# First loads of an adaLN block issued by SyncE and ScalarE in turn, and ScalarE's function table loaded behind its issues

## The chip, the cores and the metric

One core of a Trainium2 chip runs the kernel: TensorE (PE), VectorE (DVE), ScalarE (ACT), GpSimd (POOL) and SyncE (SP), which here only issues DMAs. The metric is the device time of one execution in microseconds (us), lower is better. It was 543.92 us as the median of three runs (543.61 to 544.06).

## What is computed

One transformer block whose layer norms are modulated by a condition c. The sizes are S = 2048 tokens, D = 512, 32 heads of 16, F = 1376; everything is f32. Cut to what matters:

```python
mod = (silu(c) @ w_mod).reshape(1, 6, 1, 512)
sa, ca, ga, sb, cb, gb = mod's six rows
h = layernorm(x) * (1 + ca) + sa
q, k, v = split(h @ wqkv)                 # 32 heads of 16
phi = lambda t: where(t > 0, t + 1, exp(t)) + 1e-6
kv, z = einsum("sd,se->de", phi(k), v), phi(k).sum(tokens)      # per head
x = x + ga * ((phi(q) @ kv / (phi(q) . z + 1e-6)) @ wo)
h = layernorm(x) * (1 + cb) + sb
x = x + gb * (((h @ w_gate) * (h @ w_up)) @ w_down)
```

The change touches only how the first inputs come in: x, c, and the columns of w_mod for ca and sa.

## The kernel before

The program is written in a fixed order (a manual schedule): each engine runs its instructions in the order in which the code emits them, and waits at an instruction until its operands are there. The tokens are cut into four chunks (NCH) of four tiles (NJ) of 128 tokens, the 512 features into four blocks (KD) of 128. f32 operands of the large products are split into a high and a low part (`split`, L195, the high part by ScalarE at L196, the low part by VectorE at L197), and each product is three matmuls.

**Loads (L111 to L135).** `load` takes a tile and issues one DMA of 256 KB from SyncE's queue. All loads of the first stage are emitted one after the other: four x tiles of chunk 0 (in what follows x0 to x3), c (`ct`, 2 KB), four row groups of w_mod for ca (`raw_ca`), four for sa (`raw_sa`), then the K columns of wqkv (`raw_k`), x of chunk 1, the Q and V columns, and x of chunks 2 and 3.

**The opening (L432 to L505).** TensorE starts with 24 dummy matmuls (`keep_on(24)`, L146, whose operand VectorE makes at L140 and L141), and more of them stand between the first transposes. Meanwhile

- VectorE takes the statistics of the four x tiles as they land (L244, L245); GpSimd makes rstd (L265), VectorE nmr (L269);
- ScalarE normalises a tile (`xhat`, L274) as soon as nmr is there. Between its first and second tile stands exp(-c) (`silu_exp`, L153), from which VectorE makes sc = silu(c) (L156 to L158);
- VectorE and ScalarE sum the rows of w_mod with the weights sc: acc_ca with L164 and three L166, acc_sa with ScalarE's L446, two L166, and the last row group by TensorE itself (L468);
- TensorE transposes the normalised tiles (L302), then turns acc_ca and acc_sa into columns by a product with ones (L459 for ca; L468 and L469 for sa). VectorE takes the columns out (L176, L492), makes the first modulated block (L494), and the first projection starts (K, L489, then L482 to L484).

From there the K projection, the key-value sums, Q, the attention output and the feed-forward part follow.

**ScalarE's function table.** The load of the table (ACT_TABLE_LOAD) is placed by the compiler ahead of the first ACTIVATE on ScalarE's queue, which before is that of the first `xhat`, L274.

Of the kernel before, what the change touches and what calls it, by code (L numbers as in the profile page):

```python
# [8 lines left out]
F32 = mybir.dt.float32  # L9
F32R = mybir.dt.float32r  # L10
AF = mybir.ActivationFunctionType
# [3 lines left out]
P = 128  # L15
# [9 lines left out]
def tile_adaln_block(  # L25
# [12 lines left out]
    nc = tc.nc  # L38
    ctx.enter_context(tc.manual_schedule())
    _, S, D = x.shape  # L40
    F = w_gate.shape[1]
    KD = D // P
    NJ = 4
# [9 lines left out]
    xv = x[0].rearrange("(c p j) d -> c j p d", p=P, j=NJ)  # L53
# [5 lines left out]
    wm_v = w_mod.rearrange("(p k) n -> p k n", k=KD)  # L59

    pool = lambda name, bufs, **kw: ctx.enter_context(tc.tile_pool(name=name, bufs=bufs, **kw))
    consts = pool("consts", 1)
# [14 lines left out]
    def B(tag, shape=(P, D), dt=F32):  # L77

        return T(tiles, tag, shape, dt)
# [28 lines left out]
    nc.gpsimd.memset(half, -0.5)  # L108


    def load(src, tag):  # L111
        raw = B(tag, (P, *src.shape[1:]))[:src.shape[0]]
        nc.sync.dma_start(raw, src)
        return raw

    def load_x(ch):
        return [load(xv[ch, j], "x") for j in range(NJ)]

    def load_mod(v):
        return [load(wm_v[:, k, v * D:(v + 1) * D], "raw") for k in range(KD)]  # L120

    def load_qkv(n):
        return [load(wqkv_v[k, :, n * D:(n + 1) * D], "raw") for k in range(KD)]

    xts = [load_x(0)]
    ct = consts.tile([P, KD], F32, name="ct")
    nc.sync.dma_start(ct, c[0].rearrange("(p k) -> p k", k=KD))
    raw_ca = load_mod(1)
    raw_sa = load_mod(0)
    raw_k = load_qkv(1)  # L130
    xts.append(load_x(1))
    raw_q = load_qkv(0)
    raw_v = load_qkv(2)
    xts.append(load_x(2))
    xts.append(load_x(3))  # L135

# [407 lines left out]
    def mod_load(*vs):  # L544
        raw_m.update({v: load_mod(v) for v in vs})
# [25 lines left out]
    for i in range(NT):  # L571
        ch, j = divmod(i, NJ)
# [1244 lines left out]
```

## Time and profile before

| what | before |
|---|---|
| median of three runs | 543.92 us |
| the profiled execution, its own time | 543.86 us |
| its span, first to last instruction | 542.2 us |
| instructions | 8140 |
| granted TensorE clock, mean | 1.0 |
| bytes by DMA, mean rate | 109.21 MB, 201 GB/s |

The profile is of one execution. Busy times are sums over an engine's instructions; a view by stages cuts the span at given times; the view of waits says for how long an engine stood still ahead of an instruction and what ended that; the timeline gives for each instruction, or for a run of the same ones, the start, the time from the first start to the last end, the engine, the line and the tiles. For a DMA the last number of its row is the time from its issue to its landing. A row "PEld" is a weight load on TensorE, which may run beside the matmul ahead of it. Times are counted from the start of the span.

### The profile page before, as it was taken

To read this page: it belongs to the slowest core of one execution; us is meant where nothing else is said; L and a number is where in the kernel's file an instruction comes from. 1 tells how busy PE (TensorE), PEld (TensorE's weight loads), DVE (VectorE), ACT (ScalarE), POOL (GpSimd) and SP (SyncE) were. 2 spreads that over 40 slices of the span, in tenths; PEclk is the share of its full clock that TensorE was granted. 3 is DMA by queue.
4 is the path that set the end of the run, shared out by engine and by line. 5 is a ranking of instruction groups with operands and counts; after the bars stand their busy time and mean duration, and the time that the engine had idled before them with its cause. 6 is when DMAs were issued, how large, how long until landed. Compare 5 with 4: busy or idle time off the path is not lost. (4 is left out here: it accounts for less than half of the span.)

```text
span 542.2 us, 8140 instructions
## 1 busy us (share of the span) xinstructions
PE 535.5 (99%) x2617; PEld 448.3 (83%) x2617; DVE 407.4 (75%) x688; ACT 295.9 (55%) x557; POOL 160.7 (30%) x169
## 2 busy tenths in 40 slices
PE   8999999999999999999999999999999999999997
PEld 7888787888888878878888888887788888899996
DVE  7897779999989888779765677997745554666762
ACT  3696777648587765577674545444524234353320
POOL 2001010010021220085796566749622313210000
PEclk9999999999999999999999999999999999999999
DMA  8902427220165165947879496893189999689122
GB/s 280 383 35 98 136 93 218 89 68 2 44 195 196 37 213 154 294 142 237 285 215 314 186 318 207 254 371 95 43 299 375 380 382 325 224 296 365 52 79 78
DMA packets 86395, 109.21 MB, mean 201 GB/s; under 512 B 10896, under 2 KB 41616, under 8 KB 86352
## 3 DMA queue, kind: packets, MB, share of 16 engines
q1 hardware_dynamic: 86352, 108.70, 59.8%
q8 instruction: 20, 0.33, 0.2%
q14 instruction: 23, 0.19, 0.1%
HBM read 65.93 MB, written 42.73 MB: 200 GB/s over the span
## 5 line engine op out<-in xcount | busy, mean ns | idle before, releaser
L1156 PE MATMUL bank<-h,w 128*128 128x512 f32 (+1 forms) x630 | 145.7, 390 | 0.4 <-DVE u L1218 0.3
L1156 PEld LDWEIGHTS bank<-h,w 128*128 128x128 f32 (+1 forms) x630 | 116.9, 186 | 27.1 <-DVE u L1218 0.7
L1161 ACT ACTIVATE bank<-bank 128x512 f32<-128x512 f32 (+1 forms) x30 | 17.5, 583 | 73.8 <-PE bank L1156 73.6
L197 DVE TENSOR_TENSOR kl<-u,kh 128x512 fp32r<-128x512 f32 (+1 forms) x43 | 30.6, 743 | 27.8 <-ACT kh L196 23.7
L265 POOL TENSOR_TENSOR rstd<-ve,half 128x2 f32<-128x2 f32 (+3 forms) x13 | 11.8, 910 | 109.0 <-DVE ve L264 45.0
L211 PE MATMUL bank<-w,h 128*128 128x512 f32 x104 | 40.9, 393 | 0.1
L209 PE MATMUL bank<-w,h 128*128 128x512 f32 x104 | 40.9, 393 | 0.0
L210 PE MATMUL bank<-w,h 128*128 128x512 f32 x104 | 40.6, 390 | 0.0
L1156 PE MATMUL acc<-h,w 128*128 128x512 f32 x168 | 38.7, 389 | 0.0
L197 POOL TENSOR_TENSOR w<-raw,w 128x512 fp32r<-128x512 f32 (+1 forms) x15 | 21.6, 1446 | 53.4 <-ACT w L196 47.7
L873 PE MATMUL acc<-w,xh 128*128 128x512 f32 x120 | 37.1, 390 | 0.0
L1156 PEld LDWEIGHTS acc<-h,w 128*128 128x128 f32 x168 | 31.5, 188 | 6.5
L1118 POOL TENSOR_TENSOR w<-raw,w 128x256 fp32r<-128x256 f32 (+3 forms) x22 | 24.8, 1127 | 38.3 <-ACT w L1111 34.1
L943 DVE TENSOR_TENSOR x<-acc,x 128x512 f32<-128x512 f32 x40 | 26.1, 685 | 9.9 <-PE acc L1241 8.2
L1436 PE MATMUL acc<-w,kh 128*128 128x256 f32 (+1 forms) x176 | 31.9, 284 | 0.1
L1118 POOL TENSOR_TENSOR w<-t,w 128x512 fp32r<-128x512 f32 (+1 forms) x22 | 29.9, 1357 | 0.0
L196 ACT ACTIVATE kh<-u 128x512 fp32r<-128x512 f32 (+1 forms) x43 | 24.6, 622 | 8.3 <-DVE u L1413 8.3
L1436 PEld LDWEIGHTS acc<-w,kh 128*128 128x128 f32 (+1 forms) x176 | 27.5, 192 | 0.4 <-ACT kh L196 0.3
L873 PEld LDWEIGHTS acc<-w,xh 128*128 128x128 f32 x120 | 22.5, 188 | 4.6
L416 PE MATMUL acc<-kh,xh 128*128 128x512 f32 x64 | 25.3, 395 | 0.0
L1436 PE MATMUL acc<-w,kl 128*128 128x256 f32 x88 | 25.0, 284 | 0.2 <-DVE kl L197 0.2
L1436 PE MATMUL bank<-w,kh 128*128 128x256 f32 (+1 forms) x136 | 24.7, 284 | 0.5 <-DVE x L1485 0.5
(257 smaller groups left out, 1330.0 us busy)
## 6 DMA issues: line engine op xcount, KB each, us to landing
right<-w SPq DMA_DIRECT2D x56, 256.0 KB, 3.4
w<-right SPq DMA_DIRECT2D x56, 256.0 KB, 5.1
raw<-in_w_mod_dram SPq DMA_DIRECT2D x24, 256.0 KB, 3.7
raw<-in_B_w_down_dram SPq DMA_DIRECT2D x20, 256.0 KB, 4.4
down_t<-w SPq DMA_DIRECT2D x20, 256.0 KB, 5.1
w<-down_t SPq DMA_DIRECT2D x20, 256.0 KB, 4.2
x<-in_A_x_dram SPq DMA_DIRECT2D x16, 256.0 KB, 5.4
down_b<-w SPq DMA_DIRECT2D x15, 256.0 KB, 5.2
```

The costliest lines, as they stand in the source:

```text
L196: nc.scalar.activation(h, src, AF.Copy)
L197: (low or nc.vector).tensor_tensor(l, src, f32(h), op=ALU.subtract)
L209: nc.tensor.matmul(ps, ah, bh, start=i == 0, stop=False)
L210: nc.tensor.matmul(ps, ah, bl, start=False, stop=False)
L211: nc.tensor.matmul(ps, al, bh, start=False, stop=i == n - 1)
L416: nc.tensor.matmul(tacc[k], xh[:, a:b], kh, start=first, stop=False)
L873: nc.tensor.matmul(yps[i], x, y, start=False, stop=k == KD - 1 and x is al, skip_group_check=True)
L943: nc.vector.tensor_tensor(xt[:, a:b], dn[j][:, a:b], xt[:, a:b], op=ALU.add)
L1118: sub = lambda out, x, y: (on or nc.gpsimd).tensor_tensor(out, x, f32(y), op=ALU.subtract)
L1156: mm = lambda x, y, **kw: nc.tensor.matmul(ps, x[:, k], y, skip_group_check=True, **kw)
L1161: nc.scalar.activation(out, x, AF.Copy)
L1436: nc.tensor.matmul(ps, x[:, a:b], y, start=start, stop=False, skip_group_check=True)
```

## The change

`load` gets a parameter for the issuing engine, and `load_x` and `load_mod` one for a cycle of engines. For chunk 0 of x, for raw_ca and for raw_sa the tiles 0 and 2 are issued by SyncE and the tiles 1 and 3 by ScalarE; ct is issued by ScalarE. Behind these loads in the order of the program stands a new exp of a 128x1 tile on ScalarE, which is set to zero by VectorE ahead of L140. Later loads stay with SyncE.

```diff
-    def load(src, tag):
+    ONE, TWO = (nc.sync,), (nc.sync, nc.scalar)
+
+    def load(src, tag, by=nc.sync):
         raw = B(tag, (P, *src.shape[1:]))[:src.shape[0]]
-        nc.sync.dma_start(raw, src)
+        by.dma_start(raw, src)
         return raw
 
-    def load_x(ch):
-        return [load(xv[ch, j], "x") for j in range(NJ)]
+    def load_x(ch, by=ONE):
+        return [load(xv[ch, j], "x", by[j % len(by)]) for j in range(NJ)]
 
-    def load_mod(v):
-        return [load(wm_v[:, k, v * D:(v + 1) * D], "raw") for k in range(KD)]
+    def load_mod(v, by=ONE):
+        return [load(wm_v[:, k, v * D:(v + 1) * D], "raw", by[k % len(by)]) for k in range(KD)]
...
-    xts = [load_x(0)]
+    xts = [load_x(0, TWO)]
     ct = consts.tile([P, KD], F32, name="ct")
-    nc.sync.dma_start(ct, c[0].rearrange("(p k) -> p k", k=KD))
-    raw_ca = load_mod(1)
-    raw_sa = load_mod(0)
+    nc.scalar.dma_start(ct, c[0].rearrange("(p k) -> p k", k=KD))
+    raw_ca = load_mod(1, TWO)
+    raw_sa = load_mod(0, TWO)
+    early = consts.tile([P, 1], F32, name="early")
+    nc.vector.memset(early, 0.0)
+    nc.scalar.activation(early, early, AF.Exp)
     raw_k = load_qkv(1)
```

In the changed file the lines behind this place have numbers higher by 5 (L469 is L474 there).

How the instructions stand now is shown on three engines. In each row stand the line, the operation, the tile written and what is read (the numbers behind a name tell buffers apart), the shape, and the semaphores it waits for. DMAHW0 to DMAHW7 are eight semaphores which the loads take in turn, over both queues; a load that takes one again waits for the landing of the load that had it.

The start of SyncE's queue before: x_90 to x_96 are x0 to x3, raw_100 to raw_106 raw_ca, raw_108 to raw_114 raw_sa, raw_116 the first tile of raw_k.

```order
L113 DMA x_96<-in_A_x_dram 128x512
L127 DMA ct<-in_c_dram 128x4
L113 DMA raw_100<-in_w_mod_dram 128x512
L113 DMA raw_102<-in_w_mod_dram 128x512
L113 DMA raw_104<-in_w_mod_dram 128x512
L113 DMA raw_106<-in_w_mod_dram 128x512 [waits DMAHW0_49]
L113 DMA raw_108<-in_w_mod_dram 128x512 [waits DMAHW1_49]
L113 DMA raw_110<-in_w_mod_dram 128x512 [waits DMAHW2_49]
L113 DMA raw_112<-in_w_mod_dram 128x512 [waits DMAHW3_49]
L113 DMA raw_114<-in_w_mod_dram 128x512 [waits DMAHW4_49]
L113 DMA raw_116<-in_A_wqkv_dram 128x512 [waits DMAHW5_49]
```

DMAHW0 to DMAHW4 are those of x0, x1, x2, x3 and ct; the last tile of raw_sa (raw_114) waits for ct to land. The same stretch of SyncE's queue in the changed kernel (raw_119 is the first tile of raw_k there):

```order
L115 DMA x_90<-in_A_x_dram 128x512
L115 DMA x_94<-in_A_x_dram 128x512
L115 DMA raw_100<-in_w_mod_dram 128x512
L115 DMA raw_104<-in_w_mod_dram 128x512
L115 DMA raw_108<-in_w_mod_dram 128x512 [waits DMAHW1_49]
L115 DMA raw_112<-in_w_mod_dram 128x512 [waits DMAHW3_49]
L115 DMA raw_119<-in_A_wqkv_dram 128x512 [waits DMAHW5_49]
```

Seven loads have left SyncE's queue, and with them three of its waits. The start of ScalarE's queue before, with the first tile's xhat (n_216), exp (ce), the other tiles' xhat, and the first part of acc_sa (f_176):

```order
L274 ACT_TABLE_LOAD [waits DMAHW0_49]
L274 ACTIVATE n_216<-x_90,nmr_208,rstd_207 128x512 [waits DVE_49]
L153 ACTIVATE ce<-ct 128x4 [waits DMAHW4_49]
L274 ACTIVATE n_219<-x_92,nmr_208,rstd_207 128x512 [waits DMAHW1_49]
L274 ACTIVATE n_231<-x_94,nmr_208,rstd_207 128x512 [waits DMAHW2_49,DVE_49]
L274 ACTIVATE n_233<-x_96,nmr_208,rstd_207 128x512 [waits DMAHW3_49]
L446 ACTIVATE f_176<-raw_108,sc 128x512 [waits DMAHW1_49]
```

And in the changed kernel:

```order
L115 DMA x_92<-in_A_x_dram 128x512
L115 DMA x_96<-in_A_x_dram 128x512
L129 DMA ct<-in_c_dram 128x4
L115 DMA raw_102<-in_w_mod_dram 128x512
L115 DMA raw_106<-in_w_mod_dram 128x512 [waits DMAHW0_49]
L115 DMA raw_110<-in_w_mod_dram 128x512 [waits DMAHW2_49]
L115 DMA raw_114<-in_w_mod_dram 128x512 [waits DMAHW4_49]
L134 ACT_TABLE_LOAD
L134 ACTIVATE early<-early 128x1 [waits DVE_49]
L279 ACTIVATE n_219<-x_90,nmr_211,rstd_210 128x512 [waits DVE_49]
L158 ACTIVATE ce<-ct 128x4 [waits DMAHW5_49]
```

Seven issues now stand ahead of the table load, the new exp, the first xhat and exp of c, three of them with a wait for a landing. Which landing, the readers of the tiles show: DMAHW0 is x0's and DMAHW2 x2's, as before, and ct now has DMAHW5. Who has DMAHW4 is seen on VectorE, where sc and the first step of acc_ca (f_178) are made, in the changed kernel:

```order
L161 TENSOR_SCALAR ce<-ce 128x4 [waits Activation_49]
L162 RECIPROCAL ce<-ce 128x4 [waits DVE_49]
L163 TENSOR_TENSOR sc<-ct,ce 128x4 [waits DMAHW5_49,DVE_49]
L169 TENSOR_SCALAR f_178<-raw_100,sc 128x512 [waits DMAHW4_49,DVE_49]
L274 SCALAR_TENSOR_TENSOR nmr_211<-mv_176,rstd_210 128x2 [waits Pool_49]
```

DMAHW4 belongs to raw_100, the first tile of raw_ca, so ScalarE's last issue (raw_114) waits for raw_100 to land, where SyncE's before waited for ct.

## The prediction

> **What bounds the kernel now.** I read the share of busy time first, then TensorE by stages, then who it waits for.
>
> ```profile
> PE 535.5 (99%) x2617; PEld 448.3 (83%) x2617; DVE 407.4 (75%) x688; ACT 295.9 (55%) x557; POOL 160.7 (30%) x169
> ...
> 2.00:10.30 8.30, 8.30 (x24) 1.00 0.91 294
> 10.30:15.80 5.50, 5.50 (x46) 1.00 1.06 397
> 15.80:19.00 3.20, 3.20 (x15) 1.00 1.05 377
> 19.00:530.00 511.00, 510.18 (x2471) 1.00 0.60 200
> 530.00:542.20 12.20, 8.34 (x68) 1.00 0.26 87
> ```
>
> In the stage rows the columns are the stage, its length, TensorE's busy time with its instructions, the granted clock, the DMA share and GB/s. From 2.0 us on TensorE is busy to within 0.8 us until 530; the tail (3.9 us) belongs to the last outputs, which the change does not touch. The waits by TensorE say what could still be won:
>
> ```profile
> PE acc L146 <- DVE w L141: 2.0, 1, 2.0
> PE bank L1436 <- DVE x L1485: 0.5, 1, 0.5
> PE bank L1156 <- DVE u L1218: 0.3, 1, 0.3
> PE acc L1436 <- DVE kl L197: 0.2, 1, 0.2
> PE bank L1156 <- DVE u L1184: 0.2, 1, 0.2
> ```
>
> None of these is a wait for a load. The first is the start, the others sum to 1.2 us (0.5 + 0.3 + 0.2 + 0.2) and lie far behind the change. So TensorE's own queue is the bound, and a faster start of the data alone cannot pull it forward. That queue in the first 16 us:
>
> ```profile
> 2.00 8.48 PE L146 MATMUL acc<-w 128*128 128x512 f32 x24 [2.00 <-DVE w L141]
> 10.32 1.03 PE L302 MATMUL bank<-ident,n 128*128 128x128 f32 x8
> ...
> 12.99 1.00 PE L459 MATMUL acc<-ones,f 128*128 128x64 f32 x8
> 13.80 0.48 PE L146 MATMUL acc<-w 128*128 128x512 f32 x1
> 14.12 0.33 PE L468 MATMUL acc<-sc,raw 128*128 128x64 f32 x2
> 14.28 0.39 PE L469 MATMUL acc<-ones,f 128*128 128x64 f32 x2
> ...
> 15.86 1.24 PE L489 MATMUL acc<-w,h 128*128 128x512 f32 x4
> ...
> L459 PEld LDWEIGHTS acc<-ones,f x8: 190/192/192, 12.9 to 13.7; 128*128 128x128 f32 x8
> ...
> L469 PEld LDWEIGHTS acc<-ones,f x8: 192/192/192, 14.2 to 15.7; 128*128 128x128 f32 x8
> ```
>
> The columns are start, time from the first start to the last end, engine and line. The 24 dummy matmuls (L146) fill TensorE until 10.3, whatever the loads do; then transposes, column sums and the first projection (L489) follow with no gap. What must be ready is made by ScalarE and VectorE:
>
> ```profile
> 4.39 1.28 ACT L274 ACT_TABLE_LOAD   x1 [4.39 <-DMA x<-in_A_x_dram]
> 7.34 0.81 ACT L274 ACTIVATE n<-x,nmr,rstd 128x512 f32<-128x512 f32 x1 [1.67 <-DVE nmr L269]
> 8.06 0.19 ACT L153 ACTIVATE ce<-ct 128x4 f32<-128x4 f32 x1
> 8.16 0.80 ACT L274 ACTIVATE n<-x,nmr,rstd 128x512 f32<-128x512 f32 x1
> 9.71 1.52 ACT L274 ACTIVATE n<-x,nmr,rstd 128x512 f32<-128x512 f32 x2 [0.75 <-DVE nmr L269]
> 11.33 0.72 ACT L446 ACTIVATE f<-raw,sc 128x512 f32<-128x512 f32 x1
> 14.04 0.63 ACT L196 ACTIVATE w<-raw 128x512 fp32r<-128x512 f32 x1 [1.99 <-DMA raw<-in_A_wqkv_dram]
> ...
> 8.35 0.16 DVE L156 TENSOR_SCALAR ce<-ce 128x4 f32<-128x4 f32 x1
> ...
> 9.61 4.01 DVE L166 SCALAR_TENSOR_TENSOR f<-raw,sc,f 128x512 f32<-128x512 f32 x5
> ```
>
> The chain to follow is ce (ScalarE, ends 8.25), silu on VectorE from 8.35, and the five L166, which end at 13.62 with acc_sa. L469's first weight load, the first to read acc_sa, starts at 14.2 (14.23, since its matmul starts at 14.28 and the one before at 14.12). A reader starts some 0.1 us behind its source here (ce ends 8.25, VectorE 8.35), so acc_sa has about **0.5 us of slack**. The table load ends at 5.67, and ScalarE then waits 1.67 us for nmr: the table costs nothing today.
>
> **The change, part by part.** The table load, moved ahead of data that was waited for anyway, can win nothing; that is its best case. The new memset (128x1) stands ahead of VectorE's L140; its like, a 16-element operation such as L156, takes 0.16 us, so the first dummy starts at most 0.16 us later, and and what that moves on TensorE is covered by the wait found below: nothing, and up to 0.16 us if that wait is not there.
>
> The step that matters is the seven issues that now stand on ScalarE's queue ahead of the table load, exp and xhat. The order shown with the change says what they wait for: eight DMA semaphores go round over the loads of both queues, so a load waits for the landing of the one that had its semaphore before. ScalarE's fifth issue waits for x0, the sixth for x2, and the seventh, the last tile of raw_sa, for **the first tile of raw_ca** (raw_100). The same rule can be seen at work in the trace, on SyncE:
>
> ```profile
> x<-in_A_x_dram SPq DMA_DIRECT2D x1, 256.0 KB, 3.5
> x<-in_A_x_dram SPq DMA_DIRECT2D x1, 256.0 KB, 4.1
> x<-in_A_x_dram SPq DMA_DIRECT2D x1, 256.0 KB, 5.1
> 3.13 0.43 SPq L113 DMA_DIRECT2D raw<-in_w_mod_dram  x1
> raw<-in_w_mod_dram SPq DMA_DIRECT2D x1, 256.0 KB, 4.9
> 5.81 0.33 SPq L113 DMA_DIRECT2D raw<-in_w_mod_dram  x1
> 7.32 0.80 SPq L113 DMA_DIRECT2D raw<-in_w_mod_dram  x2
> SPq L113 <- DMA x<-in_A_x_dram: 1.5, 2, 1.2
> ```
>
> The x rows are x0, x2 and x3, issued at 0.81, 1.72 and 2.18, with the time to landing last: they land at 4.3, 5.8 and 7.3. The 11th and 12th issue start at 5.81 and 7.32, right behind x2 and x3. Until now such waits stood on SyncE, which computes nothing. Now one stands ahead of everything that ScalarE does. raw_100, issued at 3.13, lands today at 3.13 + 4.9 = 8.0, later than ScalarE's first xhat begins (7.34).
>
> When will it land? It is now the third issue of SyncE's queue, where x2 stood (1.72). Early bound: with the shortest landing of any row, 3.5, it is there at 5.2. Late bound: the four x tiles still go ahead of it on the same DMA engines, and a w_mod tile of ScalarE's queue now goes beside it; a tile takes 0.65 us of the engines (256 KB at 397 GB/s), so 8.0 + 0.65 = 8.7. The landings are further apart (4.3, 5.8 and 7.3 for x0, x2 and x3) than the issues, so the transfer sets the pace, and what an earlier issue wins and the tile beside it costs I set against each other: **8.0**, as today.
>
> (The Trainium skill, DMA: Bandwidth & Descriptors, section "Issuing engines are not separate DMA queues", says that DMAs of all issuers run on the same 16 engines and that a second issuer saves only the sequencer's time. It speaks against the change. If the issue set the pace, raw_100 would land earlier by 3.13 - 1.72 = 1.4, at 6.6, and the time would be 544.5; by the rule it stays near 8.0, and 545.9 follows.)
>
> From there: the last issue starts at 8.04 (0.04 behind the landing, as 7.32 behind 7.28) and takes 0.43 as SyncE's do, so the table load starts at 8.47; it takes 1.28 (9.75); the early exp is a small ACTIVATE like ce, behind which the next starts 0.10 later (8.06 to 8.16); xhat of tile 0 starts at about 9.85 instead of 7.34. ce follows as today. **Delay of ce: 2.5 us.** How ScalarE's issues compare with SyncE's no row shows. The bounds:
>
> ```profile
> L113 SPq DMA_DIRECT2D x<-in_A_x_dram x16: 327/328/997, 0.8 to 24.8; - x16
> L146 PE MATMUL acc<-w x12: 628/628/797, 2.0 to 6.9; 128*128 128x512 f32 x12
> L146 PE MATMUL acc<-w x9: 387/389/397, 8.0 to 9.9; 128*128 128x512 f32 x9
> ```
>
> The shortest and longest issue of this form took 0.33 and 1.00 us. Only the last of the seven counts, since the six before it end in the shadow of the wait: 0.1 less or 0.57 more than my 0.43. (The dummy rows are needed below: 11 steps from 2.0 to 6.9 are 0.44 us each, 8 steps from 8.0 to 9.9 are 0.24.)
>
> What is queued behind ce: VectorE's silu, the first L164, nmr of tiles 2 and 3, and the L166; on ScalarE the xhat of tiles 2 and 3 (they wait for that nmr) and L446. All move together by 2.5, and acc_sa ends at 16.1 instead of 13.62. With the slack of 0.5 taken off, L469 and the first projection start **2.0 us later**. The other readers have more room and would give less: the column sums L459 need the third L166 (9.61 + 3 x 0.80 = 12.0) and load weights from 12.9, a slack of 0.8; the transposes of tile 0 start at 10.32 and its xhat ends at 8.15. The first split of raw_k (ScalarE, 14.04 today) is needed only with the projection; L446, ahead of it, ends 2.5 later than 12.05, at 14.55, which costs nothing.
>
> Nothing behind takes the delay up: from 19 us on TensorE idles 0.8 us in 511. SyncE's loads behind raw_w_mod wait for landings, as today. Sum: 543.86 (span 542.2 and 1.66 around it; the median of the runs is 543.92) + 2.0 = **545.9 us**.
>
> **The rivals.** First, **not slower**: raw_100 lands early because two queues fill the engines sooner. The point from which it loses nothing is a delay of 0.5 us, that is a landing at 8.0 - 2.0 = 6.0 or before; the early bound, 5.2, lies beyond it. For it: from 2 to 10.3 the loads moved 294 GB/s, later 397, so the engines had room. Against it: x3, with three tiles ahead, took until 7.3, and raw_100 has four. It gives 543.9 and no gain, since the dummies hold TensorE; a landing up to 7.1 gives at most 545.0 and is counted here. 0.28.
>
> Second, **ScalarE is held longer**: an issue there costs 1.00 (0.57 more), and raw_100 lands at the late bound (0.65 more). 2.0 + 1.2 = 3.2: 547.1. For it: raw_100 now shares the engines with a tile of the other queue, where it had x ahead and nothing beside. Against it: most issues of the form took 0.33. 0.11.
>
> Third, **TensorE's clock falls back**: the waits make gaps between 10 and 18 us, and the matmuls start slowly again. The dummy rows above show the slow pace from 2.0 to at most 8.0. Such a stretch once more costs 6 x (1 - 0.24/0.44) = 2.7 us: 548.6. Against it: the gaps are 2 us in all, and between them transposes and column sums run. 0.06. (The Trainium skill, TensorE: Matmul & The Clock Gate, Part 1, puts the clock at half after an idle window of about 3.4 us; by that rule 2 us would not do it. No run shown here has such a gap.)
>
> Fourth, **faster**: if all four later waits went, 1.2 us; 542.7. Nothing ties them to the first loads, and VectorE, not DMA, ends them. 0.03.
>
> **How the numbers follow.** The forecast has 0.52, with its own range 545.1 to 546.7 (a landing between 7.2 and 8.7, 0.1 us for the issue). The range 543.8 to 547.4 takes in the first and the second rival and leaves out the third and fourth. A measurement of this kernel can tell about 0.2% (1.1 us) from no change, so slower means above 545.0: the forecast and the second and third rivals, 0.69. Within 0.2%: the first, less a little for chance, 0.27. Faster: the fourth with that little, 0.04.
>
> **What would show it.** In the changed profile: the last raw_sa issue on ScalarE starts just behind the landing of raw_100, near 8.0; the table load near 8.5 and not at 4.4; xhat of tile 0 near 9.85, behind ScalarE's own queue and not behind nmr; ce near 10.6; the last L166 (there L171) ends near 16.1; TensorE stands still for about 2 us in all between 10.3 and L469 (there L474), and L489 (there L494) starts near 17.9. Behind that everything is moved by one amount. I am wrong if raw_100 lands before 7, if ScalarE reaches xhat by 7.9, or if the first projection starts at 15.9 and the time still moves.

## The result and the profile after

The changed kernel takes 545.51 us as the median of 6 runs (545.0 to 546.21); the kernel before took 543.67 us beside it (6 runs, 543.22 to 544.06). The ratio is 1.0034, 95% interval [1.0021, 1.0047]: slower, by about 0.34%. The profiled execution of the changed kernel took 545.52 us with a span of 543.8, the one of before 543.86 with 542.2.

ScalarE's queue at the start of the changed kernel, from its timeline (start, time from first start to last end, engine or its queue, line, operation):

```profile
0.80 0.90 ACTq L115 DMA_DIRECT2D x<-in_A_x_dram  x2
1.73 0.45 ACTq L129 DMA_DIRECT2D ct<-in_c_dram  x1
2.21 5.88 ACTq L115 DMA_DIRECT2D raw<-in_w_mod_dram  x4
8.12 1.28 ACT L134 ACT_TABLE_LOAD   x1 [8.12 <-DMA raw<-in_w_mod_dram]
9.41 0.20 ACT L134 ACTIVATE early<-early 128x1 f32<-128x1 f32 x1
9.52 0.80 ACT L279 ACTIVATE n<-x,nmr,rstd 128x512 f32<-128x512 f32 x1
10.23 0.19 ACT L158 ACTIVATE ce<-ct 128x4 f32<-128x4 f32 x1
```

The four w_mod issues take 5.88 us from the first start to the last end, because three of them wait, and the table load behind them is put down to the landing of a w_mod tile. Which tile, the views of loads by the time of issue show: the first row is raw_100, issued by SyncE at 1.72, so it landed at 1.72 + 6.0 = 7.72; the second is ScalarE's last issue, from the timeline.

```profile
raw<-in_w_mod_dram SPq DMA_DIRECT2D x1, 256.0 KB, 6.0
7.75 0.34 ACTq L115 DMA_DIRECT2D raw<-in_w_mod_dram  x1
```

VectorE and TensorE in the same timeline:

```profile
4.63 0.69 DVE L249 BATCH_NORM_STATS2 st<-x 128x6 f32<-128x512 f32 x1 [2.38 <-DMA x<-in_A_x_dram]
7.72 0.13 DVE L274 SCALAR_TENSOR_TENSOR nmr<-mv,rstd 128x2 f32<-128x2 f32 x1
10.45 0.17 DVE L161 TENSOR_SCALAR ce<-ce 128x4 f32<-128x4 f32 x1 [1.57 <-ACT ce L158]
11.58 3.78 DVE L171 SCALAR_TENSOR_TENSOR f<-raw,sc,f 128x512 f32<-128x512 f32 x5
...
2.02 7.21 PE L151 MATMUL acc<-w 128*128 128x512 f32 x24 [2.02 <-DVE w L146]
10.38 1.46 PE L307 MATMUL bank<-ident,n 128*128 128x128 f32 x8 [1.15 <-ACT n L279]
...
17.04 1.23 PE L494 MATMUL acc<-w,h 128*128 128x512 f32 x4
```

nmr is there at 7.85, yet xhat starts at 9.52: ScalarE is late, not its data. VectorE waits 1.57 us for ce, TensorE 1.15 us for the first xhat, and the first projection starts at 17.04 instead of 15.86. By stages (stage, length, TensorE's busy time, clock, DMA share, GB/s):

```profile
2.00:10.30 8.30, 7.21 (x24) 1.00 0.99 345
10.30:15.80 5.50, 5.05 (x34) 1.00 1.05 386
15.80:19.00 3.20, 3.20 (x21) 1.00 0.99 345
19.00:530.00 511.00, 510.11 (x2463) 1.00 0.60 200
```

TensorE now stands still in the opening, and no more than before behind it by this view. The loads ran faster: 345 GB/s up to 10.3 us, where it was 294. Followed matmul by matmul, the delay against the first profile is 1.2 us from 18 to 87 us, and 1.7 us from 95 us on. So a second, smaller loss of 0.5 us sits near 90 us; the last experiment comes to it.

### The profile page after: what moved, and what is told of

The parts are those of the page before. It is cut to its first block, busy times and chain, and to the rows that moved or that the text cites. A ratio compares the mean times of both kernels' runs of the same rounds, so it can differ in the third digit from the quotient of the medians.

```text
span 543.8 us, 8140 instructions
## 1 busy us (share of the span) xinstructions
PE 535.6 (98%) x2617; PEld 447.2 (82%) x2617; DVE 406.4 (75%) x689; ACT 295.8 (54%) x558; POOL 160.4 (29%) x169
## 3 DMA queue, kind: packets, MB, share of 16 engines
q10 hardware_dynamic: 1008, 1.58, 0.8%
```

## The experiments

All are edits of the changed kernel (numbers of its lines) or of the kernel before, each run beside the kernel before on the same chip. Three theories are set against the main one, that ScalarE is held by the issues that wait: A, that two queues bring the first tiles late; B, that the table load or the early exp costs; C, that the number of issues costs.

**First: the issues that wait go back to SyncE.**

```diff
-    raw_ca = load_mod(1, TWO)
-    raw_sa = load_mod(0, TWO)
+    raw_ca = load_mod(1, (nc.sync, nc.scalar, nc.sync, nc.sync))
+    raw_sa = load_mod(0)
```

> Kept of the change: x1, x3, ct and one raw_ca tile issued by ScalarE, none of which waits, and the early exp; the three loads whose issue waits for a landing go back to SyncE. Theory (ScalarE is held by its waiting issues): the table load starts near 2.7 us, xhat of tile 0 when nmr is there, 7.8 to 8.0, and the first projection at 15.9 to 16.1 us instead of 17.04; time 543.6 to 544.2. Rival A (two queues in themselves bring the first tiles late): still near 17.0, 545 or more. Rival B (the table or the early exp is the cost): near 17.0, since both still stand behind issues.

Measured: 543.37 us, ratio 1.0002 [0.9993, 1.0010]. ScalarE and TensorE in its timeline:

```profile
2.85 1.28 ACT L134 ACT_TABLE_LOAD   x1 [2.85 <-issue]
7.87 0.82 ACT L279 ACTIVATE n<-x,nmr,rstd 128x512 f32<-128x512 f32 x1 [3.53 <-DVE nmr L274]
...
15.41 1.24 PE L494 MATMUL acc<-w,h 128*128 128x512 f32 x4
```

xhat waits for nmr again, and the loss is gone, with two queues, table and early exp still there. The first projection is even 0.45 us ahead of the first profile of before, earlier than expected; the ninth experiment explains that.

**Second: only the last issue goes back.**

```diff
-    raw_sa = load_mod(0, TWO)
+    raw_sa = load_mod(0, (nc.sync, nc.scalar, nc.sync, nc.sync))
```

> The changed kernel with only its last raw_sa tile given back to SyncE, so ScalarE's last issue waits for x2 (landed 6.85) and not for the first raw_ca tile (7.72). Theory: table load near 7.3, xhat of tile 0 near 8.65, the first projection near 16.2 us, 0.85 earlier than in the changed kernel; time near 544.7. Rivals A and B: 17.0 us and 545.5, as in the changed kernel.

Measured: 544.40 us, 1.0018 [1.0009, 1.0027].

```profile
6.99 1.28 ACT L134 ACT_TABLE_LOAD   x1 [6.99 <-DMA x<-in_A_x_dram]
8.39 0.80 ACT L279 ACTIVATE n<-x,nmr,rstd 128x512 f32<-128x512 f32 x1
...
15.92 1.24 PE L494 MATMUL acc<-w,h 128*128 128x512 f32 x4
```

The landing that holds ScalarE is now an x tile's, and xhat, and the first projection, come 1.1 us earlier than in the changed kernel (0.85 was expected; the table load started at 6.99 and not near 7.3). One issue less on the queue did that, the one that waited for the latest landing.

**Third: no early exp and no memset** (the three lines of `early` removed).

> The changed kernel without the early exp and its memset; the compiler then puts the table load ahead of the first xhat, which is still behind all seven issues. Theory: xhat of tile 0 0.1 us earlier than 9.52, the first projection near 16.95 us, time near 545.4. Rival B (the early exp is the cost): back to 15.9 us and 543.7. Rival A: 17.0 us, 545.5.

Measured: 545.15 us, 1.0037 [1.0025, 1.0050]. The table load starts at 7.97, xhat at 9.26, the first projection at 16.80. The loss stays, against theory B; the early exp itself is worth its 0.1 us step.

**Fourth: the early exp moved up**, right behind the issue of ct, the same three lines ahead of `raw_ca`.

> The changed kernel with memset and early exp moved up, right behind the issue of ct, so the table is loaded between ScalarE's third and fourth issue, before any that waits. Theory: xhat of tile 0 starts right behind the last issue, near 8.15 us, 1.4 earlier than in the changed kernel; 0.8 late against before, of which 0.5 is slack: the first projection at 15.9 to 16.2 us, time 543.7 to 544.3. Rival A: 17.0 us and 545.5. Rival B (any early exp costs): more than 16.5 us.

Measured: 543.87 us, 1.0011 [1.0001, 1.0020].

```profile
2.21 1.28 ACT L132 ACT_TABLE_LOAD   x1 [2.21 <-issue]
4.65 3.33 ACTq L115 DMA_DIRECT2D raw<-in_w_mod_dram  x3
8.03 0.82 ACT L279 ACTIVATE n<-x,nmr,rstd 128x512 f32<-128x512 f32 x1 [4.33 <-DVE nmr L274]
...
15.56 1.24 PE L494 MATMUL acc<-w,h 128*128 128x512 f32 x4
```

The issues still wait (4.65 to 7.98), but xhat starts right behind the last one instead of 1.4 us later. So of the changed kernel's lateness 1.4 us is the table load and the early exp that stand behind the wait, where the table load alone stood in idle time before. The first projection is again earlier than expected (15.9 to 16.2), and the ratio is only just clear of 1.

**Fifth: the early exp alone**, in the kernel before, all loads with SyncE.

> The kernel before, with only the memset and the early exp added (all loads on SyncE). Theory: the table is loaded near 1 to 2.5 us and nothing follows from it, since xhat waits for nmr until 7.3 either way; first projection between 15.3 and 15.9 us (where in it depends on when TensorE's clock opens in that execution), time as before, 543.4. Rival B (the table or the early exp costs or gains): a difference of over 0.5 us.

Measured: 543.23 us, 0.9996 [0.9987, 1.0005]. The table is loaded from 0.80 to 2.08 us, xhat waits until 7.42 for nmr. No difference: loading the table early is worth nothing here.

**Sixth: seven issues on ScalarE, none of which waits.**

```diff
-    xts = [load_x(0, TWO)]
+    xts = [load_x(0, (nc.sync, nc.scalar, nc.scalar, nc.scalar))]
...
-    raw_ca = load_mod(1, TWO)
-    raw_sa = load_mod(0, TWO)
+    raw_ca = load_mod(1, (nc.scalar, nc.scalar, nc.scalar, nc.sync))
+    raw_sa = load_mod(0)
```

> The changed kernel with again seven issues on ScalarE ahead of the early exp, but seven of the first eight loads (x1, x2, x3, ct, three raw_ca tiles), so that none waits for a landing; x0 and the last five w_mod tiles are SyncE's. Theory (the wait holds ScalarE, not the number of issues): issues end near 4.1 us, table load near 5.4, xhat of tile 0 when nmr is there, below 8.2, first projection 15.4 to 15.9 us, time 543.2 to 544.2. Rival C (the number of issues on ScalarE or the second queue costs): above 16.5 us and 545.

Measured: 543.86 us, 1.0005 [0.9996, 1.0014].

```profile
0.80 1.37 ACTq L115 DMA_DIRECT2D x<-in_A_x_dram  x3
2.20 0.45 ACTq L129 DMA_DIRECT2D ct<-in_c_dram  x1
2.68 1.50 ACTq L115 DMA_DIRECT2D raw<-in_w_mod_dram  x3
4.21 1.28 ACT L134 ACT_TABLE_LOAD   x1 [4.21 <-issue]
7.79 0.81 ACT L279 ACTIVATE n<-x,nmr,rstd 128x512 f32<-128x512 f32 x1 [2.08 <-DVE nmr L274]
```

The same number of issues ends at 4.18 us instead of 8.09, and ScalarE is free 2 us before nmr comes. The first projection starts at 16.03, a little above the 15.9 expected (the dummies ended late, at 2.02 + 8.62 = 10.64). Theory C is out: the waits hold ScalarE, not the number of issues.

**Seventh and eighth: 20 dummies instead of 24**, once in the kernel before and once in the first experiment's kernel.

```diff
-    keep_on(24)
+    keep_on(20)
```

> The kernel before with 20 dummy matmuls ahead instead of 24. Theory (the dummies cover 0.5 us of slack in the profiled execution of before, where TensorE's clock opened late): the dummies end by 9.5 us, L469 starts as soon as acc_sa is there, near 13.75, and the first projection at 15.3 to 15.5 us instead of 15.86; time 543.0 to 543.4. If the dummies are not what holds TensorE there: 15.86 us again.

> The first experiment (four issues on ScalarE, none of them waiting, and the early exp) with 20 dummy matmuls instead of 24. Theory: VectorE's chain alone sets the start of the first projection, 15.3 to 15.5 us, whenever the clock opens; time 543.0 to 543.4, 0.1 to 0.4 below the kernel before in the median. If TensorE's clock needs the four dummies, later matmuls start slowly and the time is 544 or more.

Measured: 543.33 us, 0.9996 [0.9988, 1.0005], and 543.55 us, 1.0002 [0.9993, 1.0011]. The first projection starts at 15.40, as expected, and at 15.21, a little below the 15.3 to 15.5 expected. Neither time is clear of the kernel before, and the second missed its expectation of 0.1 to 0.4 us below.

**Ninth and tenth: both kernels once more**, unchanged, for a second profile.

> The kernel before once more, for a second profile. Theory (the opening has two bounds, TensorE's dummies when its clock opens late and VectorE's chain when it opens early): first projection between 15.3 and 15.9 us; the stage from 87 to 95 us may lose up to 0.3 us against the first profile, by the landing of the tiles turned through DRAM. Time 543.4.

> The changed kernel once more, for a second profile. Theory: first projection 7.5 us behind the start of ScalarE's first xhat, whatever TensorE's clock does, that is 16.8 to 17.2 us. Open: whether the 0.5 us that the first profile lost between 87 and 95 us comes again (then it belongs to the change) or not (then it is scatter). Time 545.0 to 545.6.

Measured: before again 542.65 us, 0.9997 [0.9987, 1.0006]; changed again 544.48 us, 1.0031 [1.0019, 1.0042], beside 543.04 us. The kernel before, second profile:

```profile
2.00 7.18 PE L146 MATMUL acc<-w 128*128 128x512 f32 x24 [2.00 <-DVE w L141]
9.02 1.03 PE L302 MATMUL bank<-ident,n 128*128 128x128 f32 x8
15.10 1.25 PE L489 MATMUL acc<-w,h 128*128 128x512 f32 x4
...
7.56 0.82 ACT L274 ACTIVATE n<-x,nmr,rstd 128x512 f32<-128x512 f32 x1 [2.23 <-DVE nmr L269]
```

and the changed kernel, second profile:

```profile
9.16 0.80 ACT L279 ACTIVATE n<-x,nmr,rstd 128x512 f32<-128x512 f32 x1
...
16.68 1.25 PE L494 MATMUL acc<-w,h 128*128 128x512 f32 x4
```

In the second profile of before the dummies end at 9.2 instead of 10.5, since they went over to their fast form earlier (the last section shows this), and the first projection starts 0.76 us sooner, below the range expected. In the changed kernel the dummies end at 9.2 and 9.3 in its two profiles, and early dummies help nothing there: the first projection follows xhat. At 16.68 it is a little below its range as well, and the time is below the 545.0 to 545.6 expected. So the opening of before has two bounds, dummies and chain, and the changed one only the chain.

**Eleventh: SyncE's queue made longer again.** Both profiles of the changed kernel lose time near 90 us. TensorE runs the key-value products of a tile there, and from the first of one tile to the first of the next it took 95.30 - 86.64 = 8.66 us before. The rows of before and then of the changed kernel, in the timeline:

```profile
86.64 0.39 PE L416 MATMUL acc<-kh,xh 128*128 128x512 f32 x1
95.30 0.39 PE L416 MATMUL acc<-kh,xh 128*128 128x512 f32 x1
```

```profile
87.81 0.39 PE L421 MATMUL acc<-kh,xh 128*128 128x512 f32 x1
97.00 0.40 PE L421 MATMUL acc<-kh,xh 128*128 128x512 f32 x1
```

That is 9.19 in the changed kernel (and 9.49 in its second profile). In this stage VectorE needs tiles that SyncE sends through DRAM and back in small pieces (`u<-first`, 16 loads), and waits for them. The view of waits between 78 and 96 us, for the kernel before, the changed kernel and the kernel of this experiment (us in total, times, longest), shows VectorE's wait:

```profile
DVE wide L338 <- DMA u<-first: 0.9, 1, 0.9
DVE wide L343 <- DMA u<-first: 1.2, 1, 1.2
DVE wide L346 <- DMA u<-first: 1.1, 1, 1.1
```

The wait is 0.3 us longer in the changed kernel. The turned tile ahead of it comes later too: VectorE starts it 84.01 - 80.33 = 3.68 us behind its kl there (L413), for 82.63 - 79.13 = 3.50 before (L408). The two make 0.5 us, which is the loss.

The DMA view of the stretch from 79 to 83 us shows the changed kernel with a transfer that the kernel before does not have there; the columns are packets, MB and share of the engines.

```profile
q14 instruction: 1, 0.01, 0.8%
```

Before, it falls between 73 and 79 us (`q14 instruction: 1, 0.01, 0.4%`), ahead of those loads, which begin at 78.93. Its kind is "instruction". SyncE's queue is seven instructions shorter in the changed kernel. The experiment adds eight:

```diff
     xts.append(load_x(3))
+    for n in range(8):
+        spare = consts.tile([P, KD], F32, name=f"spare{n}")
+        nc.sync.dma_start(spare, c[0].rearrange("(p k) -> p k", k=KD))
```

> The changed kernel with eight more loads of 2 KB (c again, into tiles that nobody reads) on SyncE behind the last x load. In the changed kernel SyncE's queue is seven instructions shorter, and its profiles show a small DMA of queue q14 (instruction) between 79 and 83 us, amid the loads of the turned tiles, where the profiles of the kernel before show none; between 87 and 95 us TensorE then loses 0.5 to 0.8 us. Theory D (the shifted instruction fetch delays these loads): with SyncE's count restored the q14 DMA is back near 76 to 78 us and that stage loses 0.0 to 0.3 us; the opening stays as in the changed kernel (first projection 7.5 us behind the first xhat); time 544.5 to 545.1, about 0.5 below the changed kernel. Rival (scatter of the landings, or the later opening itself): 0.5 to 0.8 us lost there wherever the q14 DMA falls.

Measured: 544.78 us, 1.0023 [1.0013, 1.0033]. xhat starts at 9.32, the first projection at 16.85. The DMA view from 73 to 79 us, and the key-value products:

```profile
q14 instruction: 1, 0.01, 0.3%
```

```profile
87.66 0.39 PE L424 MATMUL acc<-kh,xh 128*128 128x512 f32 x1
96.47 0.39 PE L424 MATMUL acc<-kh,xh 128*128 128x512 f32 x1
```

The transfer is back ahead of the loads (none between 79 and 83), and the stage takes 8.81 us. 0.38 of the 0.53 us are back, with the opening as late as ever; the turned tile starts 3.50 us behind kl again, and the wait of 1.1 us is the rest. The rival, that this loss follows from the late opening, falls in the profile. The fourth and sixth experiments point the same way: their first projections start at 15.56 and 16.03, and the stage still takes 9.19 and 9.32 us. The other half of the rival, scatter, is not excluded by this one profile; the order over all profiles, at the end, speaks against it. In the time it is not clear: the two intervals, [1.0013, 1.0033] and [1.0021, 1.0047], overlap.

The openings together, in us, in the order of xhat:

| kernel | first xhat | first projection | behind it |
|---|---|---|---|
| before, again | 7.56 | 15.10 | 7.54 |
| no waits, 20 dummies | 7.67 | 15.21 | 7.54 |
| no waits | 7.87 | 15.41 | 7.54 |
| table ahead of the waits | 8.03 | 15.56 | 7.53 |
| last issue back | 8.39 | 15.92 | 7.53 |
| changed, again | 9.16 | 16.68 | 7.52 |
| no early exp | 9.26 | 16.80 | 7.54 |
| changed, 8 loads on SyncE | 9.32 | 16.85 | 7.53 |
| changed | 9.52 | 17.04 | 7.52 |
| before | 7.34 | 15.86 | 8.52 |
| early exp alone | 7.42 | 15.60 | 8.18 |
| before, 20 dummies | 7.33 | 15.40 | 8.07 |
| seven issues, no wait | 7.79 | 16.03 | 8.24 |

In nine of thirteen profiles the first projection follows the first xhat by 7.52 to 7.54 us, whatever moved the xhat. The last four are held by something else: the dummies (before; seven issues), or mostly the landing of the last x tile, for which VectorE's statistics wait (0.44 of the 0.65 us more in the fifth, 0.34 of the 0.54 us more in the seventh experiment).

## Why the prediction was right, point by point

- **The wait on ScalarE's queue**: right in kind and place. The last raw_sa issue started at 7.75, 0.03 us behind the landing of raw_100 at 7.72 (8.0 predicted). Experiments one and six remove the waits, and the loss in the opening goes with them; the second shortens the last one, and 1.1 us come back. In the fourth the waits stay, and it is enough to put the table load ahead of them.
- **The cost of an issue on ScalarE**, which no row showed: it was SyncE's (four x loads in 1.81 us before, 0.45 each). The waiting one took 0.34 us (0.43 taken), the unhindered ones follow each other at 0.44 to 0.49 (0.80, 1.24, 1.73, 2.21).
- **The delay of xhat**: 9.52 instead of 9.85, so 2.2 and not 2.5 us; the early landing makes 0.3 of that.
- **acc_sa**: it ended at 11.58 + 3.78 = 15.36, not at 16.1. Of the 0.75 us, 0.3 are the delay of xhat. Another 0.23 are the five steps of the sum, which took 3.78 us where the first profile of before has 4.01 (its second has 3.78 as well), and 0.2 lie between xhat and the first of them (11.58 - 9.52 = 2.06 us for 9.61 - 7.34 = 2.27). So the first projection started at 17.04 and not near 17.9, and TensorE stood still for 1.5 us up to 15.8 (8.30 - 7.21 and 5.50 - 5.05) where about 2 were predicted.
- **The slack of 0.5 us**: right for the profiled execution, wrong as a property of the kernel. It exists only when the dummies end late. In the second profile of before they ended early, and the opening's loss there is 16.68 - 15.10 = 1.58 us with a smaller delay of xhat (1.6).
- **"Nothing behind takes the delay up"**: right that none is taken up, wrong that none is added. The stage near 90 us lost 0.53 us more, 0.38 of which came back with SyncE's queue made long again. Sum as measured: 1.18 in the opening and 0.53 there make 1.7, and the profiled executions differ by 545.52 - 543.86 = 1.66 us. So 545.9 was near the measured 545.51, partly by luck: a delay taken too long (2.0 for 1.18) stood for a second loss not foreseen.
- **The rivals.** "Not slower" was a matter of when raw_100 lands, and it did not land before 6.0 (7.72). The table is loaded behind the issues, as the change says, but at 8.12 instead of 4.39. The clock did not fall back: behind the gap of 1.15 us the dummies at 11.59 took 0.71 us for two, as they did before at 11.11. That agrees with the Trainium skill, TensorE: Matmul & The Clock Gate, Part 1, which asks for an idle window of about 3.4 us.
- **The rule weighed there**, from the Trainium skill, DMA: Bandwidth & Descriptors, section "Issuing engines are not separate DMA queues", was the better guess of the two: raw_100, issued 1.4 us earlier, landed 0.3 us earlier (7.72 for 8.03). It is not the whole of it: the loads moved 345 GB/s up to 10.3 us where it was 294.

## What to carry to other kernels

A DMA issue on a compute engine's queue was cheap here only as long as it waited for nothing: seven such issues cost nothing measurable, and one that waited for a late landing held the whole queue. So count how many loads may be in flight (eight here), and give that engine only loads below that number, or put its own work ahead of the first that waits. Before moving a setup step earlier, see whether it stands in idle time already; here the table did, and moving it behind waits made it 1.4 us of the critical chain. And where two bounds lie within half a microsecond, one profile shows only the one that won in that execution.

## What was not expected of the hardware

**The first tile comes later, the later ones sooner.** With two queues VectorE's first statistics start at 4.49 to 4.80 us in nine profiles, with SyncE alone at 3.94 to 4.34 in four. Yet where ScalarE waits for the first raw_k tile to land before it splits it, that is at 12.8 to 13.2 us in five profiles with two queues and at 13.5 to 14.0 in four with SyncE alone. Nor did an earlier issue help the small load of c: issued at 1.73 it landed 6.2 us later, at 7.9, and before, issued at 2.66, 4.8 us later, at 7.5.

**When TensorE's clock opens varies.** The slow form of the dummies lasts to 7.7 us in the first profile of before, as the first row shows; in the first profile of the changed kernel, the second row, all dummies from 5.6 us on are fast (min/median/max of one in ns, first and last start).

```profile
L146 PE MATMUL acc<-w x14: 469/628/797, 2.0 to 7.7; 128*128 128x512 f32 x14
```

```profile
L151 PE MATMUL acc<-w x15: 387/389/398, 5.6 to 8.8; 128*128 128x512 f32 x15
```

The change of pace goes with the granted clock: the trace's first record of the full clock stands at 7.87 us in the first profile of before and at 5.16 us in the changed kernel's. (The stage rows print 1.00 from 2.0 us on, because ahead of that record the trace holds none.) In the second profile of before the record stands at 5.06 us. So the end of the 24 dummies moves by more than a microsecond between executions of the same kernel (10.5 and 9.2 us in the two profiles of before).

**Instruction transfers have a place in the program.** The length of the stage near 90 us goes with the length of SyncE's queue: 8.66, 8.66, 8.71 and 8.88 us in four profiles with all loads there, 8.88 and 8.98 with four fewer, 9.12 with six fewer, 9.19 to 9.91 in five profiles with seven fewer, and 8.81 with one more. The place of the q14 transfer goes with it too. Counted from SyncE's first `u<-first` load, it starts 2.5 to 2.8 us ahead in the five profiles with all loads or one more, 0.3 us behind with four fewer, 0.8 us with six fewer and 1.5 to 1.6 us with seven fewer. That the transfer of kind "instruction" delays SyncE's small loads is the reading that fits; how it does so was not shown, and neither was that it is SyncE's own instructions that it brings.
